# RetNet attention and a hard-swish MLP in one kernel: four token pieces as 64x64 tiles, and pairs of half slices at the head of a GEMM

## The chip, the cores and the metric

The kernel runs on one core of a Trainium2 chip. TensorE (PE in the profile) multiplies; a matmul takes a stationary operand, loaded by a separate weight load (PEld), and a moving one of up to 512 columns, and writes to PSUM, of which there are eight banks of 512 fp32 values per partition. VectorE (DVE) and ScalarE (ACT) read PSUM and write SBUF. GpSimd (POOL) and SyncE (SP) issue transfers here. Each engine runs its instructions in the order in which the program lists them, and waits for others by semaphores. The metric is the device time of one execution in microseconds (us).

## The reference

```
scores = (1/8) * q @ k^T                        # 8 batches, 8 heads, 576 tokens, head size 64
ret    = scores * D,  D[i,j] = gamma_h^(i-j) for i >= j, else 0,  gamma_h = 1 - 2^(-5-h)
x      = (ret @ v), heads side by side          # 4608 tokens x 512
h      = x @ w_in                               # 512 x 2048
out    = (h * clip(h + 3, 0, 6) / 6) @ w_out    # 2048 x 512
```

q, k, v, the weights and the output are fp32 in memory. The kernel loads them as fp16 and accumulates in fp32.

## The kernel before

**Pieces.** The decay factors over token positions, so that scaled q, k and v give plain causal attention within a piece of 128 tokens, plus q times a state: the sum of k^T v over the tokens before. A piece is 128 tokens of one batch, all heads; pieces 0 to 3 are batch 0, pieces 4 to 7 batch 1, and so on. The last 64 tokens of each batch go two batches to a piece, at the end. For each piece the kernel transposes q and k (to qk), multiplies them (scores, to PSUM tile sc), masks on VectorE (to at), and adds two products in PSUM tile o: masked scores times v (`intra`) and state times q (`inter`). ACT copies o to xt, the MLP's input. The state's increment k^T v goes to tile u (`update_mm`); VectorE adds and scales it (ts).

There are two forms of this work. Pieces 0 to 7 are done as 128 tokens, with matmuls of 128 columns; a state is kept as blocks on the diagonal of a full 128x128 operand (tbd), to which ACT copies ts in two copies (lines 429 and 430). Pieces from 8 on go in pairs, as halves of 64 tokens in tiles of 64x64 of the array: `scores4`, `inter4`, `intra4`, `update4`, `outputs4`. There each half has its own state: "lo" is the state before the piece, "hi" (tm) the state after its first half (`state_half`, line 541); `state_whole` adds the second half. `inter_done` (line 490) is a copy of one element per partition on ACT behind the state matmuls.

**MLP.** A block is 512 tokens. First GEMM: 16 slices of 128 features, each four matmuls of 512 columns into one bank (`g1_mm`, line 577), then ACT (585) and VectorE (586) make the hard-swish from the bank. Second GEMM of blocks 0 and 1: `g2`, a unit is four matmuls for one group of 128 tokens; later blocks have a form with fewer products. Block 0's first two slices, and block 1's first four, are computed in column parts (`g1_columns`, line 600), since the last tokens of the block come late: 256 and 256 columns in block 0, 384 and 128 in block 1. A slice is evicted when both parts are there.

**Order.** The order on every engine is written out by hand. `put` runs a list of units and behind unit j the steps named for j. During the second GEMM of block 0, `first_step(c)` runs for pieces 3 to 8 (behind units 3, 9, 11, 13 and 14, and step 8 between the column parts of block 1). Step c transposes q and k of piece c+1 on TensorE, makes the scores of piece c, and ends piece c-1; later pieces are transposed by transfers from SP. The loads of q, k and v are issued by POOL, 11 pieces' buffers ahead; `hold` ties the loads of pieces 10 and 11 to an update.

**Banks.** PSUM tags: sc has two banks, o and tu one each, and ph four, which rotate between GEMM slices, the output tiles of `g2`, the transposes and all else that asks for `bank()`.

Of the kernel before, what the change touches and what calls it, by code (L numbers as in the profile page):

```python
# [10 lines left out]
FP32 = mybir.dt.float32  # L11
# [6 lines left out]
def kernel(  # L18
# [16 lines left out]
    nc = tc.nc  # L35
# [38 lines left out]
    def xt_of(kb):  # L74
        if kb not in xts:
            xts[kb] = big.tile([P, NCC, MBLK], FP16, tag="xr" if kb == B else "xt",
                               bufs=1 if kb == B else 2, name=f"xt_{kb}")
        return xts[kb]
# [6 lines left out]
    def bank(shape, dtype, name):  # L85
        return psum.tile(shape, dtype, tag="ph", bufs=4, name=name)

    def bank_or(tag, shape, dtype, name):
        return psum.tile(shape, dtype, tag=tag, name=name) if tag else bank(shape, dtype, name)
# [109 lines left out]
        nc.scalar.copy(gqv[:, 0], gq[:, :, None].to_broadcast([P, H, D]))  # L199

    tbd = []
    for i in range(5):
        t = const.tile([P, NPAIR, P], FP16, name=f"tbd{i}")
        if i >= EARLY:
            nc.vector.memset(t, 0.0)
        tbd.append(t)

    newest = [None]
    warmed = [0]
# [17 lines left out]

    st = {}
    later = []
    free_tbd = list(range(5))  # L230
    state_of = {}
    ts_of = {}

    def rows(i):
        return slice(i * HALF, i * HALF + HALF)
# [227 lines left out]
                    in1=mask64[:, None, None, :].to_broadcast([P, 2, NPAIR, HALF]), op=ALU.mult)  # L463
        return mask

    def inter4(cs):

        o = [psum.tile([P, 2, NPAIR, HALF], FP32, tag="o", name=f"o0_{cs[0]}"),
             bank([P, 2, NPAIR, HALF], FP32, name=f"o1_{cs[0]}")]
        written = set()  # L470
        for j, c in enumerate(cs):
            kind, b, i, _ = pieces[c]
            if kind == "rest":
                states = [ts_of[2 * b], ts_of[2 * b + 1]]
            else:
                states = [st[c]["lo"], st[c]["hi"]]
            st[c].update(o=o, j=j, written=written)
            for half in (1, 0):
                if states[half] is None:
                    continue  # L480
                for p in range(NPAIR):
                    for h2 in range(2):
                        nc.tensor.matmul(  # L483
                            o[half][rows(h2), j, p, :], states[half](h2, p),
                            st[c]["qk"][rows(h2), 0, p, rows(half)],
                            start=(half, h2) not in written, stop=False, skip_group_check=True)
                        written.add((half, h2))
                st[cs[0]]["end"] = (half, j)
# [33 lines left out]
    def update4(cs):  # L522

        cs = [c for c in cs if pieces[c][0] != "rest"]
        if not cs:
            return
        u = [psum.tile([P, 2, NPAIR, D], FP32, tag="tu", name=f"u0_{cs[0]}"),
             bank([P, 2, NPAIR, D], FP32, name=f"u1_{cs[0]}")]
        for j, c in enumerate(cs):
            kn, vs = loaded[c]["kn"], st[c]["vs"]  # L530
            st[c]["u"] = [u[0][:, j], u[1][:, j]]
            for p in range(NPAIR):
                for half in range(2):
                    for h2 in range(2):
                        nc.tensor.matmul(u[half][rows(h2), j, p, :], kn[rows(half), 2 * p + h2, :],  # L535
                                         vs[rows(half), 2 * p + h2, :],
                                         start=(j == 0 and p == 0),
                                         stop=(j == len(cs) - 1 and p == NPAIR - 1),
                                         skip_group_check=True)

    def state_half(c):

        kind, b, i, _ = pieces[c]
        if kind == "rest":
            return
        u, before = st[c]["u"], st[c - 1]["ts"] if i else None
        tm = work.tile([P, NPAIR, D], FP16, tag="tm", bufs=4, name=f"tm_{c}")
        st[c]["sum"] = ta = work.tile([P, NPAIR, D], FP32, tag="th", bufs=2, name=f"th_{c}")
        if i:
            st[c]["lo"] = lambda h2, p: before[rows(h2), p, :]  # L550
            nc.vector.tensor_tensor(out=ta, in0=u[0], in1=before, op=ALU.add)  # L551
        else:
            st[c]["lo"] = None
            nc.scalar.copy(ta, u[0])  # L554
        st[c]["hi"] = lambda h2, p: tm[rows(h2), p, :]
        nc.scalar.copy(tm, ta)  # L556

    def state_whole(c):
        kind, b, i, _ = pieces[c]
# [29 lines left out]
    def g1_bank(kb, fc):  # L589
        return bank([P, MBLK], FP32, name=f"ph_{kb}_{fc}")  # L590
# [3 lines left out]
        g1_mm(kb, ph, fc, range(NCC))  # L594
        g1_act(kb, ph, fc)

    def g1_columns(kb, fc, ph, cols):

        for dmc in range(NCC):
            newest[0] = nc.tensor.matmul(ph[:, cols], win16[:, dmc, P * fc:P * fc + P],  # L600
                             xt_of(kb)[:, dmc, cols],
                             start=(cols.start == 0 and dmc == 0),
                             stop=(cols.stop == MBLK and dmc == NCC - 1),
                             skip_group_check=True)
        if cols.stop == MBLK:
            g1_act(kb, ph, fc)

    def g1_first(kb):

        banks = [g1_bank(kb, fc) for fc in range(2)]  # L610
        for cols in (slice(0, MBLK // 2), slice(MBLK // 2, MBLK)):
            for fc in range(2):
                g1_columns(kb, fc, banks[fc], cols)

    def store(kb, mc, cols, src):
        if kb < B:
# [10 lines left out]
    def g2(kb, mc, part):  # L627
        gt = gts[kb]
        if part == 0:
            pouts[kb, mc] = bank([P, DM], FP32, name=f"pout_{kb}_{mc}")  # L630
        pout = pouts[kb, mc]
        for fc in range(4 * part, 4 * part + 4):
            nc.tensor.matmul(pout, gt[:, fc, P * mc:P * mc + P], wout16[:, fc, :],  # L633
                             start=(fc == 0), stop=(fc == NFC - 1))
        if part == 3:
            osb = work.tile([P, DM], FP32, tag="osb", bufs=4, name=f"osb_{kb}_{mc}")
            nc.scalar.copy(osb, pout)
            store(kb, mc, slice(0, DM), osb)

    KH, TH, NH = NFC // 2, MBLK // 2, DM // 2  # L640
    wts = {t: big.tile([P, KH, NH], FP16, name=f"wsum_{t}") for t in ("t1", "t2", "t3", "t4")}
# [181 lines left out]
    def load_until(c):  # L823
        while next_load[0] < NP and next_load[0] <= c:
            load(next_load[0])
            next_load[0] += 1
# [26 lines left out]
            mybir.DependencyInfo(mybir.DependencyClass.Sync, mybir.DependencyReason.DATA),  # L853
            reason="one load at a time")

    def first_step(c):


        old, new, b = c - 1 >= EARLY, c + 1 < 8, pieces[c - 1][1]
        if EARLY <= c < 8:  # L860
            scale_v(c)
        if old:
            before = state_of.get(b)
            o = bank_or(None if c == 6 else "o", [P, NPAIR, P], FP32, name=f"o_{c - 1}")
            st[c - 1].update(o=o, first=True)
            copy = intra(c - 1, copy_later=True, more=before is not None)
            added = update_mm([c - 1])
            load_until(min(c + 5, 11))
            if c + 5 in (10, 11):
                hold(c + 5, added)  # L870
            update_state(c - 1, copies_later=True)
        if new:
            q_by_pe(c + 1)
        if old and new:
            run_later(9)
        if EARLY <= c < 8:
            scores(c, 0)
        if old and before is not None:
            for p in range(NPAIR):
                nc.tensor.matmul(o[:, p, :], tbd[before][:, p, :], st[c - 1]["qk"][:, 0, p, :],  # L880
                                 start=False, stop=(p == NPAIR - 1), skip_group_check=True)
        if new:
            k_by_pe(c + 1, None if old else "tu")
        if old:
            copy()
        if c < 8:
            run_later(9)

    def transpose_q_and_load(c):

# [91 lines left out]

    def gemm1(kb, steps):

        units = {0: [lambda: g1_first(kb)]}.get(kb, [])
        done = {0: 2, 1: 6}.get(kb, 0)
        if kb == 1:

            units = [lambda: g1(1, 4, "o"), lambda: g1(1, 5, "tu")]
        put(units + [unit1(kb, f) for f in range(done, NFC)], steps)  # L990


# [2 lines left out]
    gemm1(0, {9: [(fill_gq,)]})  # L995
    order = [(mc, part) for part in range(4) for mc in range(3)] + [(3, part) for part in range(4)]
    put([unit2(0, mc, part) for mc, part in order],
        {3: [(first_step, 3)], 6: [(make_mask64,)], 4: [(weight_sums, "t1")],
         9: [(weight_sums, "t2"), (weight_sums, "t3"), (first_step, 4)],
         11: [(first_step, 5)], 13: [(first_step, 6)], 14: [(first_step, 7), (transpose_k, 8)],  # L1000
         15: [(transpose_k, 9)]})

    banks = [g1_bank(1, fc) for fc in range(4)]
    done, last = slice(0, 3 * P), slice(3 * P, MBLK)
    for fc in range(2):
        g1_columns(1, fc, banks[fc], done)
    first_step(8)
    transpose_q(8)
    for fc, cols in ((2, done), (0, last), (1, last), (3, done), (2, last), (3, last)):
        g1_columns(1, fc, banks[fc], cols)  # L1010
    gts.pop(0)


# [82 lines left out]
```

## Time and profile before

| | us |
|---|---|
| median of 3 runs | 291.39 (291.15 to 292.52) |
| the profiled execution | 291.25 |
| its span, first to last instruction | 289.5 |
| PE busy | 281.3 (97%) |
| DVE busy | 227.7 (79%) |
| ACT busy | 167.4 (58%) |
| POOL busy | 106.7 (37%) |

The granted TensorE clock is 1.00 throughout. A timeline line gives start, length, engine, source line, operation, output and inputs, the tile of the array used (rows*columns), the operand's shape and how many instructions are merged; brackets give idle time before it and what ended that. Matmuls overlap in the array, so their lengths add up to more than the time that passes: the distance from one group's start to the next is the cost. The second GEMM of block 0 runs from 31.00 to 51.05, and the first GEMM of block 1 begins at 51.05.

### The profile page before, as it was taken

What the parts mean: (1) busy time and instruction counts of PE and PEld (TensorE: products, weight loads), DVE (VectorE), ACT (ScalarE), POOL (GpSimd) and SP (SyncE); (2) the same over time, 40 slices, a digit from 0 to 9 for tenths busy, and PEclk for the clock granted to TensorE, in tenths of its full rate; (3) what the DMA queues carried; (4) which work ended last, traced back from release to release, by engine and by line L of the source; (5) the groups of instructions that cost most, each with busy time, mean ns of one, the idle gap of its engine ahead of it and who ended that gap; (6) DMA issues with size and microseconds to landing.
All of it is one profiled execution on the core that took longest, in us unless ns stands there. A gap on an engine that the chain in (4) does not pass through costs nothing.

```text
span 289.5 us, 8362 instructions
## 1 busy us (share of the span) xinstructions
PE 281.3 (97%) x3500; PEld 175.2 (61%) x3500; DVE 227.7 (79%) x378; ACT 167.4 (58%) x298; POOL 106.7 (37%) x133
## 2 busy tenths in 40 slices
PE   7889999999999999999999999999999999999994
PEld 2554446544454687468746874587458745874583
DVE  4867657798769997999789978997899588627871
ACT  6658437774468545764586447744864287338720
POOL 8962567358534333333333334454650000000000
PEclk9999999999999999999999999999999999999999
DMA  9999999999999989999999999989991250121014
GB/s 137 153 199 203 192 157 220 167 124 150 154 198 172 161 86 135 175 113 93 121 157 144 92 117 173 136 85 121 161 150 38 75 111 0 38 75 36 0 40 110
DMA packets 156534, 35.94 MB, mean 124 GB/s; under 512 B 143792, under 2 KB 155440, under 8 KB 156496
## 3 DMA queue, kind: packets, MB, share of 16 engines
q0 software_dynamic: 115232, 18.23, 95.7%
q1 hardware_dynamic: 40816, 16.79, 30.0%
q8 instruction: 27, 0.44, 0.6%
q10 hardware_dynamic: 448, 0.39, 0.4%
q14 instruction: 11, 0.09, 0.1%
HBM read 36.70 MB, written 9.44 MB: 159 GB/s over the span
## 4 chain that ended last, share of the span: by engine, by line
PE 84%; DMA 9%; POOL 4%; DVE 1%; issue 0%; POOLq 0%
PE ph L577 37%; PE x L718 14%; PE z L718 9%; PE pout L633 6%; DMA wout<-in_moe_w_out_dram 5%; PE y L718 5%; DMA qv<-in_q_dram 4%; PE o L483 3%; POOL qv L103 2%; PE sc L450 2%; PE o L504 1%; PE u L535 1%; POOL kn L103 1%; PE ph L600 1%; POOL win L130 1%; PE xtu L718 1%
## 5 line engine op out<-in xcount | busy, mean ns | idle before, releaser
L577 PE MATMUL ph<-xt,win 128*128 128x512 f16 x552 | 120.8, 379 | 0.2 <-DMA win<-in_moe_w_in_dram 0.2
L585 ACT ACTIVATE u<-ph,cb 128x512 f32<-128x512 f32 x144 | 98.4, 688 | 26.3 <-PE ph L577 24.5
L586 DVE SCALAR_TENSOR_TENSOR gt<-u,ph 128x512 f16<-128x512 f32 x144 | 95.7, 684 | 22.0 <-ACT u L585 20.7
L577 PEld LDWEIGHTS <-win 128*128 128x128 f16 x552 | 53.9, 98 | 64.0 <-DMA win<-in_moe_w_in_dram 0.7
L103 POOL DMA_DIRECT2D kn<-in_k_dram x40 | 34.2, 855 | 38.7 <-PE ph L577 12.8
L103 POOL DMA_DIRECT2D qv<-in_v_dram x40 | 34.0, 850 | 37.0 <-PE ph L577 16.7
L718 PEld LDWEIGHTS <-sum_s 128*128 128x128 f16 x448 | 42.7, 98 | 5.3
L103 POOL DMA_DIRECT2D qv<-in_q_dram x38 | 32.1, 846 | 29.7 <-PE z L718 8.0
L718 PEld LDWEIGHTS <-gt 128*128 128x128 f16 x336 | 32.0, 98 | 5.5
L633 PE MATMUL pout<-wout,gt 128*128 128x512 f16 x128 | 29.5, 379 | 0.0
L686 POOL DMA_DIRECT2D out_dram<-osb x1 | 0.6, 620 | 69.4 <-DVE osb L739 69.4
L718 PE MATMUL x<-wsum_t,sum_s 128*128 128x256 f16 x192 | 22.9, 273 | 0.0
L556 ACT CAST tm<-th 128x256 f16<-128x256 f32 x24 | 9.7, 405 | 20.1 <-DVE th L551 20.0
L633 PEld LDWEIGHTS <-gt 128*128 128x128 f16 x128 | 11.9, 98 | 13.0
L456 DVE TENSOR_TENSOR at<-sc,mask 128x1024 f16<-128x1024 f32 x14 | 17.0, 1216 | 1.9 <-PE sc L450 1.9
L674 DVE TENSOR_TENSOR sum_s<-gt 128x1024 f16<-128x1024 f16 (+1 forms) x21 | 18.1, 863 | 0.2
L332 DVE TENSOR_TENSOR qv<-qv,gqv 128x1024 f16<-128x1024 f16 x26 | 17.8, 683 | 0.0
L514 ACT CAST xt<-o 128x512 f16<-128x512 f32 x28 | 15.0, 585 | 4.2 <-PE o L504 4.2
L567 DVE TENSOR_TENSOR ta<-u,th 128x256 f32<-128x256 f32 x24 | 10.2, 424 | 6.2 <-ACT th L554 5.2
L718 PE MATMUL z<-wout,sum_s 128*128 128x256 f16 x112 | 14.5, 274 | 0.0
L718 PE MATMUL y<-wout,gt 128*128 128x256 f16 x112 | 14.3, 273 | 0.0
L718 PE MATMUL z<-wsum_t,sum_s 128*128 128x256 f16 x112 | 13.6, 273 | 0.0
(119 smaller groups left out, 268.8 us busy)
## 6 DMA issues: line engine op xcount, KB each, us to landing
out_dram<-osb SPq DMA_DIRECT2D x32, 256.0 KB, 3.1
kn<-in_k_dram POOLq DMA_DIRECT2D x32, 128.0 KB, 5.4
qv<-in_v_dram POOLq DMA_DIRECT2D x32, 128.0 KB, 5.3
qv<-in_q_dram POOLq DMA_DIRECT2D x30, 128.0 KB, 7.1
wout<-in_moe_w_out_dram POOLq DMA_DIRECT2D x4, 512.0 KB, 15.3
win<-in_moe_w_in_dram POOLq DMA_DIRECT2D x3, 512.0 KB, 11.6
qf<-in_q_dram SPq DMA_DIRECT2D x2, 256.0 KB, 3.5
win<-in_moe_w_in_dram POOLq DMA_DIRECT2D x2, 256.0 KB, 6.8
```

The lines of the kernel that those rows point to most:

```text
L103: loaded[c]["dma"].append(nc.gpsimd.dma_start(dst[p0:p0 + n], src[b, :, s0:s0 + n, :].rearrange("h s d -> s h d")))
L332: scaled = nc.vector.tensor_tensor(out=qv, in0=qv, in1=gqv, op=ALU.mult)
L456: nc.vector.tensor_tensor(out=at.rearrange("t a j p s -> t (a j p) s"), in0=sc.rearrange("t a j p s -> t (a j p) s"), in1=mask64[:, None, ...
L514: nc.scalar.copy(xt_at(cs[0], 0, 2 * P).rearrange("e p (j x s) -> e p j x s", j=2, x=2) [:, :, :, half, :], o[half].rearrange("e j p s -> ...
L556: nc.scalar.copy(tm, ta)
L567: nc.vector.tensor_tensor(out=ta, in0=st[c]["u"][1], in1=st[c]["sum"], op=ALU.add)
L577: newest[0] = nc.tensor.matmul(ph, win16[:, dmc, P * fc:P * fc + P], xt_of(kb)[:, dmc, :], start=(dmc == 0), stop=(dmc == NCC - 1))
L585: nc.scalar.activation(u, ph, ACTF.Relu, bias=cb[:, 0:1], scale=1.0 / 6.0)
L586: nc.vector.scalar_tensor_tensor(out=gts[kb][:, fc, :], in0=u, scalar=1.0, in1=ph, op0=ALU.min, op1=ALU.mult)
L633: nc.tensor.matmul(pout, gt[:, fc, P * mc:P * mc + P], wout16[:, fc, :], start=(fc == 0), stop=(fc == NFC - 1))
L674: nc.vector.tensor_tensor(out=s(which)[:, c0:c1], in0=x(), in1=y(), op=op)
L718: newest[0] = nc.tensor.matmul(dst, left()[:, c, P * u:P * u + P], right[:, c, :], start=(first and c == 0 and (u == 0 or name not in whol ...
```

## The change

Pieces 4 to 7 take the 64x64 form, one piece at a time. `first_step` becomes `single_step`: step c issues the state matmuls of piece c-1, the scores of piece c, the transposes of piece c+1, the output of piece c-1 and the update of piece c. The step of piece 7 moves from behind unit 14 to behind unit 15, with the last output tile's copy and store (`g2_out`) inside it; piece 7's state matmuls come behind the first pair of slices, in the two banks of tag sc, and its output behind the second. The value scaling of piece 4 moves ahead of two weight sums. For piece 4 the first half's state is copied by VectorE (`alone`). The fifth tbd tile and its memset go.

The column parts become pairs: two slices over the same 256 columns share a bank, and one ACT and one VectorE instruction evict both. Block 0's slices 0 and 1 and block 1's slices 0 to 7 are done so. In block 1 the first 256 columns of all eight come first, with piece 7 between them.

```diff
-    def inter4(cs):
-        o = [psum.tile([P, 2, NPAIR, HALF], FP32, tag="o", name=f"o0_{cs[0]}"),
-             bank([P, 2, NPAIR, HALF], FP32, name=f"o1_{cs[0]}")]
+    def inter4(cs, tag="o"):
+        if tag == "sc":
+            both = psum.tile([P, 2, 2, NPAIR, HALF], FP32, tag=tag, name=f"o_{cs[0]}")
+            o = [both[:, 0], both[:, 1]]
+        else:
+            o = [psum.tile([P, 2, NPAIR, HALF], FP32, tag=tag, name=f"o0_{cs[0]}"),
+                 bank([P, 2, NPAIR, HALF], FP32, name=f"o1_{cs[0]}")]
...
-    def state_half(c):
+    def state_half(c, alone=False):
...
-            nc.scalar.copy(ta, u[0])
+            if alone:
+                nc.vector.tensor_copy(ta, u[0])
+            else:
+                nc.scalar.copy(ta, u[0])
...
-        nc.scalar.copy(tm, ta)
+        nc.scalar.copy(tm, u[0] if alone and not i else ta)
...
+    def g1_pair(kb, fc, cols):
...
+        ph = bank([P, 2, MBLK // 2], FP32, name=f"ph_{kb}_{fc}_{cols.start}")
+        for i in range(2):
+            for dmc in range(NCC):
+                newest[0] = nc.tensor.matmul(
+                    ph[:, i], win16[:, dmc, P * (fc + i):P * (fc + i) + P],
+                    xt_of(kb)[:, dmc, cols], start=(i == 0 and dmc == 0),
+                    stop=(i == 1 and dmc == NCC - 1), skip_group_check=True)
+        u = work.tile([P, 2, MBLK // 2], FP32, tag="moeu", bufs=3, name=f"u_{kb}_{fc}_{cols.start}")
+        nc.scalar.activation(u, ph, ACTF.Relu, bias=cb[:, 0:1], scale=1.0 / 6.0)
+        nc.vector.scalar_tensor_tensor(out=gts[kb][:, fc:fc + 2, cols], in0=u, scalar=1.0,
+                                       in1=ph, op0=ALU.min, op1=ALU.mult)
...
-        if part == 3:
-            osb = work.tile([P, DM], FP32, tag="osb", bufs=4, name=f"osb_{kb}_{mc}")
-            nc.scalar.copy(osb, pout)
-            store(kb, mc, slice(0, DM), osb)
+        if part == 3 and (kb, mc) != (0, MBLK // P - 1):
+            g2_out(kb, mc)
+
+    def g2_out(kb, mc):
+        osb = work.tile([P, DM], FP32, tag="osb", bufs=4, name=f"osb_{kb}_{mc}")
+        nc.scalar.copy(osb, pouts[kb, mc])
+        store(kb, mc, slice(0, DM), osb)
...
+    def single_step(c, meanwhile=None):
+        old, cur, new = c > EARLY, c < 8, c + 1 < 8
+        if cur and old:
+            scale_v(c)
+        if old:
+            inter4([c - 1], "o" if cur else "sc")
+            inter_done([c - 1])
+        if meanwhile:
+            meanwhile()
+        if cur:
+            mask = scores4([c])
+        if new:
+            mask()
+            q_by_pe(c + 1)
+            k_by_pe(c + 1, None if old else "o")
+            if old:
+                end_pair([c - 1])
+        if cur:
+            added = update4([c])
+            if old:
+                load_until(min(c + 5, 11))
+                if c + 5 in (10, 11):
+                    hold(c + 5, added)
+            state_half(c, True)
+            if not new:
+                mask()
+                end_pair([c - 1])
+            state_whole(c)
...
-        {3: [(first_step, 3)], 6: [(make_mask64,)], 4: [(weight_sums, "t1")],
-         9: [(weight_sums, "t2"), (weight_sums, "t3"), (first_step, 4)],
-         11: [(first_step, 5)], 13: [(first_step, 6)], 14: [(first_step, 7), (transpose_k, 8)],
-         15: [(transpose_k, 9)]})
+        {3: [(q_by_pe, EARLY), (k_by_pe, EARLY, "tu")], 4: [(weight_sums, "t1")],
+         6: [(make_mask64,), (scale_v, EARLY)],
+         9: [(weight_sums, "t2"), (weight_sums, "t3"), (single_step, 4)],
+         11: [(single_step, 5)], 13: [(single_step, 6)],
+         14: [(transpose_k, 8)],
+         15: [(single_step, 7, lambda: g2_out(0, 3)), (transpose_k, 9)]})
...
+    for fc in range(0, 8, 2):
+        g1_pair(1, fc, lo)
+        if fc == 0:
+            single_step(8)
+        if fc == 2:
+            end_pair([7])
+            transpose_q(8)
```

In block 1's list of units, four pairs over the second 256 columns take the place of slices 4 and 5; the units from slice 8 on follow as before.

## The prediction

> **What bounds the kernel now.** I read the page first, for which engine has no idle time, then the waits of TensorE after 59 us (the answer is empty: it waits for nothing that the trace shows), and last TensorE's timeline through the stretch that the change touches.
>
> The page, engine shares:
>
> ```profile
> PE 281.3 (97%) x3500; PEld 175.2 (61%) x3500; DVE 227.7 (79%) x378; ACT 167.4 (58%) x298; POOL 106.7 (37%) x133
> ```
>
> TensorE is the bound, and from 59 us on it has no gap until its last matmul. So what the change is worth is read at one point: when TensorE begins slice 8 of block 1's first GEMM, now at 58.97 us (55.52 plus 16 matmuls at the pace below). Whatever moves that point moves the end by as much.
>
> TensorE's timeline (start, length, line, operands, tile, count):
>
> ```profile
> 40.68 0.41 PE L265 MATMUL trq<-dq,qv 128*64 128x128 f16 x8 [0.21 <-DMA qv<-in_q_dram]
> 41.03 0.40 PE L343 MATMUL sc<-qk 64*128 64x128 f16 x8
> 41.36 0.40 PE L256 MATMUL trk<-ident,kn 128*128 128x128 f16 x4
> 41.59 1.89 PE L633 MATMUL pout<-wout,gt 128*128 128x512 f16 x8
> 43.41 0.41 PE L372 MATMUL o<-at,qv 128*64 128x128 f16 x8
> 43.66 0.29 PE L394 MATMUL u<-qv,kn 128*64 128x64 f16 x8
> 43.78 0.39 PE L265 MATMUL trq<-dq,qv 128*64 128x128 f16 x8
> 44.11 0.40 PE L343 MATMUL sc<-qk 64*128 64x128 f16 x8
> ...
> 44.67 1.89 PE L633 MATMUL pout<-wout,gt 128*128 128x512 f16 x8
> ...
> 47.98 1.03 PE L633 MATMUL pout<-wout,gt 128*128 128x512 f16 x4
> 49.15 0.41 PE L372 MATMUL o<-at,qv 128*64 128x128 f16 x8
> ...
> 50.18 1.03 PE L633 MATMUL pout<-wout,gt 128*128 128x512 f16 x4
> 51.05 1.46 PE L600 MATMUL ph<-xt,win 128*128 128x384 f16 x8
> ```
>
> Lengths overlap, so a group costs the time from its start to the next group's start. The pace of 512 columns is 0.2158 us (64 matmuls from 83.84 to 97.65). Eight from 41.59 end at 43.32, and the next group, in another tile shape, starts at 43.41: a change of tile shape costs 0.09. The steps between the GEMM units now cost: step 4, 40.31 to 41.59, 1.28 (40.31: 24 matmuls after 35.13); step 5, 43.32 to 44.67, 1.35; step 6, 46.40 to 47.98, 1.58; step 7, 48.84 to 50.18, 1.34; step 8, 52.35 to 53.14, 0.79. Behind step 8 there is a wait too: from 53.14 to the first whole slice at 55.52, 8 matmuls at 0.1625 (384 columns, from 51.05 to the next group at 52.44 less one shape change) and 16 at 0.056 (128 columns) are 2.19, and 2.38 go by, so 0.19 goes to waiting for piece 7's copy into xt. With 0.28 at 40.31 for q of piece 5, and 0.22 at 48.84 for a mask (DVE's L347 ends at 49.09), some 0.7 us of this stretch is waiting. That is all there is to remove besides work.
>
> **The change, part by part.** What 64x64 tiles cost is shown where pieces 8 and 9 are done in pairs, and what 256 columns cost in block 0:
>
> ```profile
> 65.97 0.45 PE L535 MATMUL u<-qv,kn 64*64 64x64 f16 x32
> 66.25 0.46 PE L450 MATMUL sc<-qk 64*64 64x64 f16 x32
> 66.64 5.35 PE L633 MATMUL pout<-wout,gt 128*128 128x512 f16 x24
> 71.93 0.44 PE L483 MATMUL o<-qk,tm 64*64 64x64 f16 x16
> ```
>
> ```profile
> 16.76 1.92 PE L600 MATMUL ph<-xt,win 128*128 128x256 f16 x16
> ```
>
> ACT's timeline, for the order in which banks are given:
>
> ```profile
> 40.51 0.59 ACT L637 COPY osb<-pout 128x512 f32<-128x512 f32 x1 [4.43 <-PE pout L633]
> ```
>
> Thirty-two take 0.28, of which 0.02 is the start; so 16 take 0.13, or 0.15 as the first after a shape change. Thirty-two that leave for full tiles take 0.39: leaving costs 0.11 more, and I take 0.12 (the nearest row), with 0.09 and 0.15 as ends. L483's sixteen take 0.27 (next row at 72.20), so a piece's state matmuls take 0.25, and 0.14 for piece 4, which has only half of them. The q group takes 0.24 (0.33 less 0.09), the k group 0.23.
>
> Step 4 becomes scores, q, k, update: 0.09+0.15+0.12+0.24+0.09+0.23+0.09+0.15+0.12 = 1.28. Scores of piece 4 now run while q of piece 5 lands (40.64), so that wait is covered. Against 1.28: 0.
>
> Step 5, state, scores, q, k, output, update: 0.09+0.14+0.13+0.12+0.24+0.09+0.23+0.09+0.15+0.13+0.12 = 1.53, against 1.35: +0.18. Two shape changes are new.
>
> Step 6, with all state matmuls: 1.64. Here I expect a wait. The update's second bank comes from the four of tag ph; three GEMM outputs and the transposes rotate there. That the longest free slot is given is borne out at 40.68: q of piece 5 starts while ACT still copies out the bank whose last use is the newest (the row at 40.51, to 41.10). By that order the update of piece 6 gets the bank of q of piece 7. Its copy ends 0.17+0.04+0.59+0.05 = 0.85 after the q group, and TensorE is there after k, a change, and the output, 0.56 later: 0.29 of waiting. Ends: 0 (another slot) and the first rival. Behind the waiting update on TensorE stands unit 14 and all that follows, so this wait counts in full, as does the next. 1.93 against 1.58: +0.35. In step 5 the same order gives the last output tile q's bank, reached 0.81 later: 0.04.
>
> Step 7 moves behind unit 15 and loses the wait for the mask: state 0.25, scores 0.13, update 0.13, output 0.13, changes 0.09+0.12, and a wait: the output may write only after ACT's one-element copy (0.16, line 495) of what the state matmuls left: 0.19+0.05+0.16+0.05 = 0.45, of which 0.26 is covered. 1.04 against 1.34: -0.30. Ends of that wait: 0 and 0.2. Queued behind that copy on ACT is the last output tile's copy, now issued in step 7; its bank is wanted by the second pair, 1.6 us later. The step passes the transpose of k of piece 8 on SP (off TensorE's path until 66.25) and the store of that tile.
>
> Step 8 and piece 7's end: 0.09+0.25+0.12 and 0.09+0.15+0.12 = 0.82, against 0.79+0.19: -0.16. Its two banks are those of piece 7's scores, whose mask must be done; DVE's four operations (0.42, 0.46, 0.60, from like rows) end as TensorE arrives, so 0 to 0.1. The wait for xt goes: two pairs of slices, 1.75, lie between, and the two half copies end some 0.5 before the second column half begins. What is late next would be that.
>
> Slices 0 to 7: 64 matmuls of 0.1094 (16 from 16.76 to the next group at 18.51) are 7.00; now 16 of 0.1625, 16 of 0.056 and 16 of 0.2158 are 6.95: +0.05.
>
> Costed at nothing: block 0's pairs (the same matmuls in the same order; the wait at 20.63 for win stands behind them); evictions (0.69 on ACT and 0.68 on DVE per pair of 0.875, as per slice now); the value scaling of piece 4, 0.42 on DVE, moved into 4.87 of idling for wout before 38.89; the memset gone at 4.96, followed by 1.82 of idling; ACT's step work, 2 half copies, 1 tm copy and 0.16 for the two tbd copies and one xt copy; the transposed q of piece 8, scaled 1.4 us later, with transposes landing in 5.0 and the first use after 66.25; loads 10 and 11, held by an update some 1 to 2 us later, while POOL is anyway behind earlier landings there.
>
> Sum: 0+0.18+0.04+0.35-0.30-0.16+0.05 = +0.16, and 0.04 for the mask: +0.2 us. In this ledger the 64x64 tiles save matmul time and pay it back in shape changes, and two waits replace three. The profiled execution took 291.25 (span 289.5 and 1.75 around it); 291.45 then, and the median is 0.14 above that execution: 291.6.
>
> **Rivals.** First, slower: the update's bank is the one that the step's own output copies have just freed. In step 5 TensorE then waits from 0.13 after the output until two copies of 0.41, queued behind the copies of q and k, are done, about 1.4 us; in step 6 about 1.1 beyond the wait I count. +2.5: 294.1. It decides from 1.3 us together. Against it stands the order seen at 40.68.
>
> Second, slower: a lone piece's sixteen do not run four abreast. Two abreast as in L394 (8 in 0.12), 192 matmuls cost 2.9 instead of 1.5 and the time is 293.0; one after the other, 0.03 each, 248 cost 7.5 instead of 2.3: 296.8. Against it: the 32 in 0.28, though always in longer runs. The Trainium skill (TensorE: Matmul & The Clock Gate, Part 1, on the gap of 56 ns) says that starts of matmuls never come closer than about 25 ns; by that, 248 would take an estimated 6.2 us. The trace disagrees for 64x64 tiles, with 9 ns per matmul at 65.97.
>
> Third, faster: shape changes cost nothing more where weights of the next shape are loaded ahead, and no wait appears. Then 21 changes at some 0.1, 2.2 in all, and 0.6 of waits fall away: 288.8. Against it: 0.09 to 0.12 at every change shown.
>
> Fourth, the waits are not removed (a landing or copy just shifts with the step): +0.3 to +0.7, 292.1, within no change.
>
> **How the numbers follow.** 0.5% is 1.46 us, about what a measurement of this kernel can tell from no change. Forecast and fourth rival, within it: 0.84 (0.72 and 0.12). First 0.06, second 0.02, and 0.03 for some other copy that arrives over a microsecond late at piece 7: slower 0.11. Third 0.05. The forecast's own range: no waits and cheap exits give -0.5, dear exits (nine times 0.03) and both waits doubled +0.8: 290.9 to 292.4. With part of the rivals, 290.8 to 292.8.
>
> **What would show it.** Right: slice 8 of block 1 begins within 0.5 us of 58.97; the new groups of 16 take 0.13 to 0.15; TensorE waits some 0.3 for a bank in step 6 and 0.2 for line 495's copy in step 7; no wait at 40.3 for q. Wrong: a gap above 1 us between the steps, a lone group of 16 above 0.2, or waits after 59 us where there are none now.

## The result, and the profile after

The changed kernel takes 293.94 us (median of 5 runs, 293.69 to 294.5), the kernel before 291.39 beside it. The ratio is 1.0085 (95% interval 1.0058 to 1.0113): slower by 0.85%, outside the range forecast. Ratios here and below leave out executions that are over 1.5% above the fastest of their kernel. The profiled execution took 294.18, span 292.4.

The page after: the span, the shares, the granted clock by slices, and the queues.

```profile
span 292.4 us, 8689 instructions
...
PE 283.0 (97%) x3656; PEld 178.4 (61%) x3656; DVE 228.2 (78%) x382; ACT 167.0 (57%) x304; POOL 106.7 (36%) x133
...
PEclk9999999799999999999999999999999999999999
...
q0 software_dynamic: 115232, 18.23, 90.6%
q1 hardware_dynamic: 40816, 16.79, 28.4%
q8 instruction: 28, 0.46, 0.7%
```

TensorE executes 156 matmuls and 156 weight loads more, and is busy 1.7 us longer. There is a dip in its clock in the eighth slice. The last line is a queue that carries instructions, not data. It was on the page of before too, and I had passed over it:

```profile
q8 instruction: 27, 0.44, 0.6%
```

Executions of both kernels begin with different clocks, so that the first GEMM starts at 16.7 us in some and at 18.5 in others. I therefore compare stages. From the end of unit 9 (where step 4 begins) to slice 8 of block 1 is the stretch of the prediction's ledger; behind it comes the rest, up to the last matmul.

| us | unit 9 ends | slice 8 begins | stretch | slice 8 to last matmul |
|---|---|---|---|---|
| before | 40.31 | 58.97 | 18.67 | 226.10 |
| after | 39.84 | 61.81 | 21.98 | 226.10 |

The whole loss, 3.3 us, lies in the stretch. (The 0.47 that the shown execution after is ahead at unit 9 is no gain of the pairs: in another execution of the old code, b_p96 below, block 0's first GEMM takes the same 13.85 us as in after, not 14.24.) TensorE's waits and its timeline, after:

```profile
PE u L536 <- issue: 1.7, 1, 1.7
```

```profile
39.93 0.32 PE L447 MATMUL sc<-qk 64*64 64x64 f16 x16
40.18 0.41 PE L262 MATMUL trq<-dq,qv 128*64 128x128 f16 x8
...
40.85 0.32 PE L536 MATMUL u<-qv,kn 64*64 64x64 f16 x16
41.10 1.90 PE L638 MATMUL pout<-wout,gt 128*128 128x512 f16 x8
...
43.98 0.32 PE L505 MATMUL o<-at,qv 64*64 64x64 f16 x16
44.12 0.30 PE L536 MATMUL u<-qv,kn 64*64 64x64 f16 x16
44.39 1.89 PE L638 MATMUL pout<-wout,gt 128*128 128x512 f16 x8
...
47.38 0.32 PE L505 MATMUL o<-at,qv 64*64 64x64 f16 x16
47.52 0.56 PE L536 MATMUL u<-qv,kn 64*64 64x64 f16 x15
49.74 0.19 PE L536 MATMUL u<-qv,kn 64*64 64x64 f16 x1 [1.66 <-issue]
49.86 2.45 PE L638 MATMUL pout<-wout,gt 128*128 128x512 f16 x8
```

Step 4 goes as computed. In step 6 fifteen of the update's sixteen matmuls run, then TensorE stands for 1.66 us before the last. Its fifteen neighbours write the same banks with the same operands, so no bank and no operand can be late for that one alone. "issue" is the profile's word for a wait that it can't explain. The chain of waits around it:

```profile
47.16 0.59 ACT qk L269
47.76 0.04 issue
47.80 0.29 PE u L536 x13
48.09 1.66 issue
49.74 0.19 PE u L536
```

The first two lines are the bank wait that the prediction expected (ACT's copy of q of piece 7): it is there, 0.24 us. The fourth is something else. And behind it the eight matmuls of units 14 and 15 last 2.45 us instead of 1.90. Windows of after, columns: window and length, busy time (count) of PE, weight loads, DVE, ACT and POOL, granted clock, DMA share, GB/s:

```profile
51.00:54.50 3.50, 3.50 (x73) 2.15 (x72) 1.28 (x4) 1.28 (x5) 1.87 (x3) 0.51 2.30 158
```

So the loss has two parts, a stall and a half clock from 51.1 to 54.5 behind it.

**What the stall is.** TensorE's program arrives by that instruction queue, in packets of 16384 bytes. One packet answers to 256 instructions (64 bytes each): before, 3500 matmuls and 3500 weight loads are 27.3 times 256, after 28.6, and the page counts 27 and 28. No record says which instruction begins a block, so I take the matmul that stood still, row 960 in the order of TensorE's program, as a border, with another every 256 rows ahead of it and behind it (192, 448, ...); the experiments below test that. From the trace's records of the packets and of the matmuls (times in us):

```
kernel  block at row  block ahead begins  its packet      it runs
before   960           46.58              47.21 to 48.17  56.17
before  1216           56.17              58.98 to 59.86  70.75
before  1728           74.17              79.01 to 80.01  81.70
after    960           43.18              47.47 to 48.43  49.74  stalled
after   1216           49.74              54.21 to 55.74  57.34
```

The packet for a block comes after the block ahead of it has begun, here 0.6 to 4.8 us later; it takes about 1 us, and the first instruction runs 1.2 us or more after its end. In after the 256 instructions ahead of row 960 ran in 4.7 us (43.18 to 47.90, the start of the last one), the packet began 4.29 after the first of them, and 4.29 + 0.96 + 1.3 is more than 4.7. Before, the 256 ahead of its row 960 lasted 9.6 us. What could delay the packet is seen in the DMA queues between 44 and 50 us, after (busy tenths in 40 slices, then packets, MB and share by queue):

```profile
DMA  9999999999999999999999999999999999999999
...
q0 software_dynamic: 4560, 0.58, 150.1%
q1 hardware_dynamic: 422, 0.77, 39.4%
q8 instruction: 1, 0.02, 1.0%
```

The one instruction packet stands among thousands of the loads of k, q and v. But full queues alone do not settle when it comes. Before, they were as full in the same window, and its packet of row 960 came 0.63 us after the block ahead:

```profile
q0 software_dynamic: 4922, 0.62, 162.3%
```

That lag is counted from a matmul in the array, and packets of some blocks come before it (up to 5.03 us, after, row 5824). Counted from the matmul 32 places ahead of it instead, no packet of any run comes sooner than 0.89 us. So the request seems to go out when TensorE's program is some 30 matmuls ahead of its array (an estimate; no record shows the request). Counted so, the packet of row 960 took 3.46 us before and 6.49 after.

### The profile page after: what moved, and what is told of

Its sections match the earlier page's. It is cut to its first block, busy times and chain, and to the rows that moved or that the text cites. A ratio compares the mean times of both kernels' runs of the same rounds, so it can differ in the third digit from the quotient of the medians.

```text
span 292.4 us, 8689 instructions
## 1 busy us (share of the span) xinstructions
PE 283.0 (97%) x3656; PEld 178.4 (61%) x3656; DVE 228.2 (78%) x382; ACT 167.0 (57%) x304; POOL 106.7 (36%) x133
## 4 chain that ended last, share of the span: by engine, by line
PE 94%; ACT 2%; DMA 1%; issue 1%; DVE 1%
PE ph L582 40%; PE x L726 14%; PE pout L638 10%; PE z L726 9%; PE y L726 5%; PE ph L611 3%; PE o L484 3%; PE sc L447 2%; PE u L536 2%; PE o L505 2%; PE xtu L726 1%; PE xo L726 1%; DMA qf<-in_q_dram 1%; PE trq L262 1%; ACT qk L254 1%
## 5 line engine op out<-in xcount | busy, mean ns | idle before, releaser
L582 PE MATMUL ph<-xt,win 128*128 128x512 f16 x536 | 117.2, 379 | 0.0
L590 ACT ACTIVATE u<-ph,cb 128x512 f32<-128x512 f32 x134 | 92.0, 687 | 24.0 <-PE ph L582 23.8
L591 DVE SCALAR_TENSOR_TENSOR gt<-u,ph 128x512 f16<-128x512 f32 x134 | 89.6, 684 | 18.9 <-ACT u L590 17.5
L582 PEld LDWEIGHTS <-win 128*128 128x128 f16 x536 | 52.4, 98 | 61.7 <-issue 0.2
L561 ACT CAST tm<-th 128x256 f16<-128x256 f32 x27 | 11.0, 407 | 20.4 <-DVE th L553 20.2
L572 DVE TENSOR_TENSOR ta<-u,th 128x256 f32<-128x256 f32 x28 | 11.9, 424 | 7.9 <-ACT th L559 5.2
```

The costliest lines, as they stand in the source:

```text
L561: nc.scalar.copy(tm, u[0] if alone and not i else ta)
L572: nc.vector.tensor_tensor(out=ta, in0=st[c]["u"][1], in1=st[c]["sum"], op=ALU.add)
L582: newest[0] = nc.tensor.matmul(ph, win16[:, dmc, P * fc:P * fc + P], xt_of(kb)[:, dmc, :], start=(dmc == 0), stop=(dmc == NCC - 1))
L590: nc.scalar.activation(u, ph, ACTF.Relu, bias=cb[:, 0:1], scale=1.0 / 6.0)
L591: nc.vector.scalar_tensor_tensor(out=gts[kb][:, fc, :], in0=u, scalar=1.0, in1=ph, op0=ALU.min, op1=ALU.mult)
```

## The experiments

The theory (F, for fetch): TensorE runs 64x64 tiles faster than its own program comes in while loads fill the queues. The rivals: the steps' own order and waits cost it (the expectations call this B, for bank); the pairs of slices do; or the clock drops first and the rest follows.

**1 and 2. The borders moved.** Nothing changes but the number of the matmuls with which TensorE is warmed up at the start, and so the place of each border.

```diff
-    warm(7, MBLK)
+    warm(43, 80)     # a_p36: 72 instructions more
+    warm(15, 240)    # a_p8: 16 more
```

> The changed kernel with its first warming of TensorE as 43 matmuls of 80 columns in place of 7 of 512, about the same time on zeros: 72 more instructions of TensorE before everything else. Theory F (fetch): in the trace of the changed kernel TensorE stands still for 1.74 us before the last of piece 6's update matmuls, which is instruction 960 of its program, waiting for nothing that the profile shows; packets of 16384 bytes on the instruction queue come once per 256 instructions, and this one ran at 47.47, 4.3 us after instruction 704. TensorE ran these 256 instructions in 4.8 us and was there before its next block. With 72 more ahead, the block's border lies 72 instructions earlier in the steps, and the 256 before it hold two more output units and take about 5.9 us, so the stall shrinks to 0 to 0.7 us, moves to step 6's transposes, and the time is 290.9 to 292.0. Theory B (bank): the sixteenth update matmul waits for something of its own step; the stall stays there and the time is 293.9.

> The changed kernel with the first warming as 15 matmuls of 240 columns: 16 more instructions of TensorE ahead. F: the stall of some 1.7 us moves forward by 8 matmuls and their 8 weight loads, to behind the seventh or eighth of piece 6's sixteen update matmuls. B: it stays before the sixteenth. Time in both about as the changed kernel, 293.5 to 294.5.

Measured: a_p36 294.07 (292.88 to 298.19), ratio 1.0057 (1.0012 to 1.0103); a_p8 298.07, one run. One of TensorE's waits in a_p36, then its timeline; and its waits on "issue" in a_p8:

```profile
PE o L484 <- issue: 1.3, 1, 1.3
```

```profile
48.31 0.58 PE L536 MATMUL u<-qv,kn 64*64 64x64 f16 x16
...
54.36 0.28 PE L484 MATMUL o<-qk,ts 64*64 64x64 f16 x5 [1.35 <-issue]
```

```profile
PE o L505 <- issue: 1.9, 1, 1.9
...
PE u L536 <- issue: 0.8, 1, 0.8
...
PE pout L638 <- issue: 0.5, 1, 0.5
```

In a_p36 the update of piece 6 runs through: the stall there is gone. The time is not, which is a miss of my expectation: the next border, row 1216, now falls into step 8, its packet begins 4.33 us after the block ahead, and TensorE stands for 1.54 us between two matmuls of one group, at a granted clock of 1.00 throughout. The stretch takes 20.43. In a_p8 both borders stall, the first eight matmuls earlier within the same group, exactly the shift; so does a third, at row 1984, by 0.46 us, which I had not foreseen. The time of a_p8 is a miss as well (293.5 to 294.5 expected): against after, its first GEMM begins 1.7 us later, its stretch is 1.6 us longer with the second stall, and what follows 0.6. The stall moves with the count of instructions, not with the work. No bank, operand or copy can move a stall in this way, and since TensorE stalls in a_p36 at full clock, and in after before the clock drops, the clock isn't the cause either.

**3. Before, with borders moved.** The old code, 192 instructions more at the start.

```diff
-    warm(7, MBLK)
+    warm(103, 32)
```

> The kernel before with the first warming as 103 matmuls of 32 columns: 192 more instructions of TensorE ahead, nothing else. F: block borders fall where, in its trace, 256 instructions run from 79.7 to 82.7 us, 3.0 us, while packets of the instruction queue in that part came 4.1 to 4.8 us after the border and took 1.0; TensorE stands still there for 2 to 3.6 us and the time is 293 to 296. B: no step is changed, so nothing changes: 291.1 to 291.7.

Measured: 298.7 (297.82 to 299.07), ratio 1.0215 (1.0149 to 1.0282). The stretch takes 18.38, but in block 1's second GEMM, which the change never touches, the timeline has:

```profile
87.49 2.72 PE L633 MATMUL pout<-wout,gt 128*128 128x512 f16 x6 [3.64 <-issue]
90.00 2.27 PE L577 MATMUL ph<-xt,win 128*128 128x512 f16 x8
```

A stall of 3.64 us at row 1984, whose packet lay at 85.20 to 86.17, and a half clock from 87.4 to 90.8. The kernel before had the same weakness and was only lucky in where its borders lay. The mechanism is as expected; the time is above what I gave for it. From slice 8 to the last matmul it is 231.46 instead of 226.10: 3.64 of stall, and 1.7 for 3.41 us at half clock, which I had not counted in full. Another 1.5 us lie ahead of the stretch, where this execution's second GEMM begins at 32.47 instead of 31.00.

**4 and 5. Room in the queues.** The changed kernel, with the loads of later pieces held until the update of piece 6: from piece 8 on (a_hold), from piece 9 on (a_hold9).

```diff
             if old:
-                load_until(min(c + 5, 11))
-                if c + 5 in (10, 11):
-                    hold(c + 5, added)
+                if c == 6:
+                    load_until(11)
+                    hold(8, added)     # a_hold9: hold(9, added)
...
-    load_until(10)                     # a_hold9: load_until(8)
     gemm1(0, {9: [(fill_gq,)]})
```

> The changed kernel with the loads of pieces 8 to 11 held until piece 6's update, instead of 10 and 11 by an update each. F: with fewer loads in the queues the instruction packet after instruction 704 comes within 1 to 2 us instead of 4.3, and the stall of 1.74 us is gone or under 0.5; the late loads may cost elsewhere, behind 60 us. B with loads as the cause is excluded by where the stall lies; by B the stall at the sixteenth matmul stays.

> The changed kernel with the loads of pieces 9 to 11 held until piece 6's update; piece 8's go as before. F: loads of piece 8 alone stand in the queues when instruction 704 asks for the block from 960 on, so its packet comes some 2 to 3 us later instead of 4.3, and the one from 1216 on about 1; stalls of 0 to 0.6 us instead of 1.74. With pieces 8 to 11 held, VectorE's wait for piece 10 held TensorE up for 2.7 us behind 60 us; 2.6 us earlier that should be gone or under 0.5. Time 291.0 to 292.3, against 293.9 for the changed kernel: what the steps in 64x64 tiles are worth by the ledger of the prediction, +0.2. B: as the changed kernel, 293.9.

Measured: a_hold 296.67, one run; a_hold9 293.94 (293.18 to 294.45), ratio 1.0057 (1.0034 to 1.008). The queues between 44 and 50 us in a_hold, and its timeline at the place of the stall:

```profile
DMA  9995554332799983979941000000000000000000
...
q1 hardware_dynamic: 377, 0.67, 30.2%
q0 software_dynamic: 312, 0.04, 10.3%
q8 instruction: 1, 0.02, 1.0%
```

```profile
49.40 0.58 PE L536 MATMUL u<-qv,kn 64*64 64x64 f16 x16
49.92 1.90 PE L638 MATMUL pout<-wout,gt 128*128 128x512 f16 x8
51.75 0.31 PE L484 MATMUL o<-qk,tm 64*64 64x64 f16 x8
```

With the loads out of the queues the packets of rows 960 and 1216 begin 1.84 and 0.95 us after the block ahead, not 4.29 and 4.47, and a_hold does not stall: update, unit 14 and step 7 follow without a gap at full clock. In a_hold9 they begin 2.70 and 1.13 after, and a rest of the stall is left. Its update and, from a run below, that of a_hold9t, where the packet begins 2.81 after, against 0.58 in a_hold:

```profile
49.34 0.75 PE L536 MATMUL u<-qv,kn 64*64 64x64 f16 x16
```

```profile
47.73 0.83 PE L536 MATMUL u<-qv,kn 64*64 64x64 f16 x16
```

The sixteenth matmul, row 960, starts 0.19 and 0.28 us after the fifteenth, where a_hold has 0.02. The profile lists no wait for it, since it counts idle time from the fifteenth's modelled end, 0.19 after its start. The stretch takes 18.89 in a_hold and 19.06 in a_hold9. So it is the loads that delay the packet, the stall shrinks with the delay, and without it the steps cost what the ledger said. The total of a_hold9 is a miss (291.0 to 292.3 expected): what was taken from the queues is missing later. The waits of TensorE in a_hold and the timeline of VectorE in the same kernel:

```profile
PE ph L582 <- DVE gt L617: 2.7, 2, 1.9
```

```profile
62.15 0.69 DVE L329 TENSOR_TENSOR qv<-qv,gqv 128x1024 f16<-128x1024 f16 x1 [2.56 <-DMA qv<-in_v_dram]
62.76 1.28 DVE L617 SCALAR_TENSOR_TENSOR gt<-u,ph 128x512 f16<-128x512 f32 x2
```

VectorE waits for v of a piece whose load was held, with the eviction of a GEMM slice queued behind. From slice 8 to the last matmul it is 229.78 and 227.50 instead of 226.10.

**6 and 7. The pairs and the order alone.** b_pairs is the kernel before with the pairs of slices only. b_order adds what else of the change needs no 64x64 tile: piece 4's scores ahead of q of piece 5, step 7 behind unit 15, step 8 behind the second pair (and `warm(17, 210)`).

```diff
-    units = [lambda: g1(1, 4, "o"), lambda: g1(1, 5, "tu")]
+    units = [lambda fc=fc: g1_pair(1, fc, hi) for fc in range(0, 8, 2)]
...
+    for fc in range(0, 8, 2):
+        g1_pair(1, fc, lo)
+        if fc == 0:          # b_order: fc == 2
+            first_step(8)
```

> The change's second part alone: pairs of slices over 256 columns in blocks 0 and 1, pieces 4 to 7 as 128 tokens as before. By the prediction's ledger 0.05 dearer in matmuls, and the wait of 0.19 for piece 7's copy into xt goes: -0.1 us. 32 more instructions of TensorE from block 1 on, in a stretch where 256 take over 6 us (by the trace of the kernel before), so F sees no stall of more than 0.5: 291.0 to 291.9. If the pairs carry the loss, 293 or more.

> The pairs, pieces 4 to 7 as 128 tokens, and what else the change reorders: scores of piece 4 ahead of q of piece 5, and the step of piece 7 behind unit 15, with step 8 behind the second pair; first warming as 17 matmuls of 210 columns (20 more instructions), so that no 256 instructions run in under 3 us where packets are late. The waits of 0.28, 0.22 and 0.19 us go, matmuls cost 0.05 more: slice 8 of block 1 begins 0.6 us sooner, 290.6 to 291.0. By F no stall from fetching above 0.3. If the order of steps carries the loss, 293 or more.

Measured: b_pairs 291.79 (290.32 to 292.8), ratio 0.998 (0.9952 to 1.0009), stretch 18.24; b_order 291.44 (290.43 to 292.71), ratio 0.9979 (0.9955 to 1.0004), stretch 18.02. Against the 18.67 of before the stretch is shorter by 0.43 and 0.65 us, so the pairs and the moved steps carry none of the loss. Of this 0.28 is the wait for q of piece 5, which the traced execution of b_p96, unaltered in this stretch, lacks too (18.38); against that one the gains are 0.14 and 0.36. b_order's time lies above what was expected (290.6 to 291.0). It is still the best version of this study: by the ratios it beats the changed kernel; against the kernel before, the interval just reaches 1.

**8 and 9. A later issue of held loads, and the changed kernel again.** a_hold9t is a_hold9 with the step that issues the loads of pieces 12 and 13 moved from unit 2 to unit 4 of block 1's GEMM; a_again is the changed kernel, unaltered, beside it.

```diff
-              2: [(transpose_q_and_load, 10)], 5: [(transpose_k, 11)], 7: [(transpose_q, 11)],
-              4: [(load_next,)], 6: [(load_next,)], 9: [(load_next,)]})
+              5: [(transpose_k, 11)], 7: [(transpose_q, 11)],
+              4: [(transpose_q_and_load, 10), (load_next,)], 6: [(load_next,)], 9: [(load_next,)]})
```

> As the run that holds the loads of pieces 9 to 11 until piece 6's update, with the scaling and transpose of q of piece 10 two units later (behind unit 4 of block 1's first GEMM): there VectorE waited 1.7 us for v of piece 10, and TensorE 1.1 us behind it. F: from unit 9 of block 0's second GEMM to slice 8 of block 1 19.0 us again (18.67 before, 21.98 in the changed kernel), from slice 8 to the last matmul 226.1 to 226.6 (227.5 with the wait), so 1.0 to 2.0 us under the changed kernel run beside it, and within 1 us of the kernel before. B or the clock as the cause: as the changed kernel beside it.

> The changed kernel itself, beside the run with held loads. F: the same borders, so TensorE stands still again before instruction 960, or before 1216 (piece 7's output), for 1 to 2.5 us together, with or without a stretch at half clock behind it: 21 to 22 us from unit 9 to slice 8. If the half clock were the loss, a profile without it would show about 20 us there.

Measured: a_hold9t 294.49 (292.29 to 295.23), ratio 1.0037 (1.0006 to 1.0068); a_again 294.96 (294.55 to 296.39), ratio 1.007 (1.0047 to 1.0092). The longest waits of TensorE in a_hold9t:

```profile
PE warm L213 <- DVE cb L151: 1.2, 1, 1.2
PE sc L340 <- ACT qk L254: 1.0, 2, 0.7
PE trq L262 <- ACT qv L127: 0.4, 1, 0.4
PE u L536 <- DVE gt L591: 0.3, 1, 0.3
```

Behind the warm-up stages nothing is left but the 0.28 us at row 960 and this last wait of 0.3; the stretch takes 19.14, and 226.96 follow. This is the shortest of its ten executions (292.29 of a median of 294.49), so it shows the version at its best; what the others lost was not traced. In a_again the stall is back at the same matmul (1.7 us, row 960, packet 48.09 to 49.02, running at 50.52), the half clock too, and the stretch takes 22.05: the stall belongs to the kernel, not to one execution. As a time a_hold9t is a miss: 0.5 us under a_again, where 1.0 to 2.0 were expected, and 1.8 above the kernel before. The intervals of a_hold9t and a_again overlap, so a_hold9t is not shown to be better as a whole.

## Why the prediction was wrong

The ledger held. In a_hold, where nothing stalls, the stretch takes 18.89 against 18.67 before: +0.22, where the sum said +0.20. (Part of that agreement is the choice of the execution: against the 18.38 of b_p96, which lacks the wait for q of piece 5, it is +0.51.) By its steps, where the choice does not enter:

| step | prediction | measured |
|---|---|---|
| 4 | 1.28 | 1.26 (after) |
| 5, with 0.04 for q's bank | 1.57 | 1.55 (after) |
| 6, with 0.29 for q's bank | 1.93 | 1.92 (a_hold); the wait 0.24 (after) |
| 7 | 1.04 | 1.08 (a_hold) |
| 8 and piece 7's end | 0.82 | 0.86 (a_hold) |
| slices 0 to 7 | 7.00 | 7.00 (a_hold) |

(Step 6 in a_hold, for one: it begins a shape change ahead of 48.09 and unit 14 begins at 49.92.) Sixteen lone matmuls do take 0.14 (43.98 to 44.12), so the second rival falls; shape changes still cost (0.09 in after, from unit 13's end at 46.12 to 46.21), so the third does; q of piece 5 is covered at 40.18, so the fourth does. The first rival gave 294.1, close to what came, but by bank waits of 1.4 and 1.1 us in steps 5 and 6; step 5 has none and step 6 only the 0.24. It hit the number by luck, with a mechanism that did not occur. The bank wait that the forecast itself counted, 0.29, was right.

What failed is the step "Costed at nothing", with the ledger's assumption that only a bank, an operand or a transfer of data can hold TensorE. It left out what the change does to TensorE's own program: 312 instructions more, and the densest of them in the stretch where the loads fill the queues. Of the 3.09 us between after and a_hold (21.98 less 18.89), 1.82 is the stall (from the first group behind unit 13 to unit 14: 46.21 to 49.86 against 48.09 to 49.92) and 1.27 the half clock behind it (units 14 and 15 +0.55, step 7 +0.32, the first pair +0.40, each by the start of its group and the next). These are not two independent prices. In a_p36 the clock stays at 1.00, and the block that follows stalls for 1.54 instead, since TensorE, running faster, gets to the border sooner; the one execution of after with a mean clock of 1.000 took 293.85, only 0.33 less than the profiled one, as that would have it, though it left no trace. The sign that I named for being wrong, "a gap above 1 us between the steps", is what appeared, a matmul short of where I put it.

The kernel before could have told it. Its page has the queue, its count divides into 256 instructions a packet, and its trace has three borders, at rows 1472, 1728 and 2240, that ran 1.68 to 1.76 us after their packet's end. Where a packet held TensorE up, the first instruction ran 1.2 to 1.6 us after its end (1.22 at row 960 of a_hold9t, 1.55 at row 1216 of a_p8): these three were under half a us from stalling. The bound would have been: a border that TensorE reaches t after the one ahead of it is safe when t is above the packet's lag, its transfer and what follows it, 4.8 + 1.0 + 1.3, some 7 us in a loaded stretch. (Only the 1.3 needs the later runs; by before alone it is at most 1.68.) By the ledger's own rows step 5, two units and step 6 are 152 matmuls, 304 instructions with their weight loads, in 4.9 us (1.53, 1.73 and 1.64). The price would have been about 2 us (7.1 less 4.9), and the forecast a slower kernel. Measured were 1.82 for the stall and 1.27 for the clock.

The Trainium skill (Runtime: NRT & Kernel Launch, Instruction fetch mechanics) states the unit: instruction memory is refilled in blocks of 16 KiB, 256 instructions, by the sequencer's own DMA queue, while the current block runs. The trace agrees with both numbers. It also says that the cost of crossing a boundary is "mostly hidden"; here that fails, with 1.66 us in after and 3.64 in b_p96.

What stays open: what a_hold9t's longer executions lose; why the packet of row 960 came so much sooner before than after, with the queues full in both; and whether any order of the loads leaves room for both the packets and the data with 64x64 tiles in this stretch. Three were tried. Two moved the lateness to the data (TensorE waits 2.7 us for it in a_hold, 1.1 in a_hold9); the third, a_hold9t, keeps 0.28 us of the stall, and even its best execution takes 0.86 us more behind slice 8.

## What to carry to other kernels

An engine's program is a transfer like any other. Where a change replaces few large matmuls by many small ones, count its instructions between two borders of 256, and compare the time in which they run with the lag of an instruction packet in that stretch, its transfer and the time until it is usable. A wait that the profile puts down to "issue", in the middle of a group of like matmuls, is the sign; to test it, shift all borders by some instructions at the start, and see whether the stall moves with them.

## What the runs showed of the hardware

- An instruction packet for TensorE (16384 bytes, 256 instructions) takes 0.9 to 1.5 us in most places (2.48 once, in a_again), and where TensorE stalled for one, the first instruction ran 1.31 (after), 1.32 (b_p96), 1.36 (a_p36), 1.50 (a_again) and 1.27 to 1.55 us (a_p8) after the packet's end.
- It comes about one block ahead, and loads in the queues delay it: with the queues empty it began 0.95 us after the block ahead of it (a_hold), with full ones up to 5.27 (b_pairs, row 1728). Where long matmuls surround a border it can begin up to 5.03 us before that block's first matmul runs (after, row 5824); never sooner than 0.89 us after the matmul 32 places ahead of it (before, row 5824).
- A stall of 1.66 us was followed, 1.3 us after its end, by a granted clock of one half for 3.41 us (after; in a_again 1.73 and 1.1), and stalls of 3.64 (b_p96) and 1.94 (a_p8) by the same at once; after the 1.35 of a_p36 and the 0.76 of a_p8 the clock stayed at 1.00.
- Moving instructions alone, with no change of the work in question, cost up to 2.15% (b_p96). Of the 6.57 us between its traced execution and that of before, 5.36 lie behind slice 8, with the stall: part of what a small change measures can be the place of its borders.
